# Attention denominators: weighted sums on ScalarE and GpSimd ahead of two matmul rounds, with M and the reciprocal moved later

## The chip, the cores and the metric

The kernel runs on one core of a Trainium2 chip. The metric is the device time of one execution in microseconds (us). A profile of one execution belongs to each kernel; it gives the busy time of each engine, the chain of work that ended last, and each instruction's start and duration. In its lines PE is TensorE's matmuls, PEld its weight loads, DVE is VectorE, ACT is ScalarE, POOL is GpSimd, SP is SyncE, which issues most DMAs, and SPq its DMA queue. L256 is line 256 of the kernel.

## What is computed

The input is x, 2048 tokens of 640 numbers in bfloat16. Two blocks are mixed by a gate per token:

```python
g = _sigmoid((x * gate_w).sum(-1, keepdims=True))
return g * a + (1 - g) * b
```

Block a is linear attention with 32 heads of 20 numbers. The change is in its denominators `den`:

```python
phi = lambda t: jnp.where(t > 0, t + 1, jnp.exp(t)) + 1e-6
pq, pk = phi(q), phi(k)
kv = jnp.einsum("bhsd,bhse->bhde", pk, v)
z = jnp.einsum("bhsd->bhd", pk)
num = jnp.einsum("bhqd,bhde->bhqe", pq, kv)
den = jnp.einsum("bhqd,bhd->bhq", pq, z)[..., None] + 1e-6
o = num / den
```

For every token and head, den is the sum over the head's 20 numbers of pq times z, where z is the sum of pk over all tokens. Block b is a mixer and an MLP: x1 = x + shift(gelu(layernorm(x) @ w1)) @ w2, then x1 + gelu(layernorm(x1) @ w3) @ w4. The shift moves the four quarters of the features by 1, -1, 2 and -2 tokens.

## The kernel before, in words

Nothing is reordered by a scheduler: each engine works its instructions in the order in which the program issues them, and waits by semaphores for what they need. So an instruction that waits holds up all that stand behind it on its engine. All matmul results go to PSUM through `pair()` (L71), a pool of four pairs of banks: a fifth matmul group waits until an earlier pair has been read out. The tokens are taken in 16 chunks of 128 or in four tiles of 512 (`NT`, `TS`). In order:

1. Keys (L206 to L234): k for each chunk, then phi into `pk`. Queries (`q_unit`, L237): q transposed, in five chunks j of 128 features, then phi into `pqT[:, j, :]`. Chunk j holds every fifth feature, so that a head's 20 numbers lie on four partitions of each of the five chunks.
2. `g_unit(j)` (L313), five units: 32 matmuls of `pk` with x give the product from which kv is made; the last column of the second half, `pt[:, 1, HD:HD + 1]`, is z for the 128 features of chunk j. ScalarE copies the product to `gs`; VectorE multiplies the mask `hmask` (which partition belongs to which head) with z into `zbd[:, j, :]`; SP transposes `gs` into `gT`. Between the units VectorE works out layernorm statistics (`ln1_stat`), GpSimd 1/sqrt of the variance (`ln1_rstd`, two instructions, L288 and L289), VectorE applies it (`ln1_apply`, L308), and SP transposes the result into `lnxT`, which W1 reads.
3. Two small memsets on GpSimd (L400, L401) write the first and last columns of `hsT`, then `w1_unit(0, ...)` (L347): three units, each of one or two chunks of W1 for tile 0, with a gelu on ScalarE (L356, L359) into `hsT`. The last unit's result is spread by four VectorE copies (L362).
4. `kv_unit` (L366) makes kv from `gT`, masked on VectorE into `kvT`. Then the first unit of W1 for tile 1, and the denominators: `den_mm` (L252) has 20 matmuls, five chunks by four tiles, with `zbd[:, j, :]` as 32-column weights; the four tiles go to four groups of 32 partitions. `den_evac` (L260) adds 1e-6 on VectorE, `den_recip` (L265) takes the reciprocal there.
5. `m_unit(g)` (L382), six units, M = kv times wo, copied out by ScalarE into `mst`, two of W1's units between them; `m_store` (L389) writes M to DRAM, and `m_load` reads it back in another arrangement into `m_sb`.
6. `w2_unit(0, cc)` (L428) for the four chunks of tile 0: ten matmuls, then VectorE adds x and takes statistics; `ln2_rstd` on GpSimd, `ln2_apply` (L448) on VectorE and a transpose on SP.
7. W1 for tile 2; after its first unit `r_spread` (L269): four VectorE copies and four DMAs that spread the reciprocals to all partitions (`rb`). Then `m_load`, the load of `w4_sb`, `scale_t(0)` (L275, VectorE multiplies pq of tile 0 by `rb`), W1 for tile 3, and the long rest: W3, W2, attention output (`att_unit`, L461) and W4 for tile after tile.

`xT` (x transposed) is read last by the queries. The pool that holds it, `st1`, is closed at L406, and the space is used again for `w4_sb` and others.

Of the kernel before, what the change touches and what calls it, by code (L numbers as in the profile page):

```python
# [7 lines left out]
ACT = mybir.ActivationFunctionType  # L8
# [8 lines left out]
def kernel(  # L17
# [14 lines left out]
    P = 128  # L32
# [57 lines left out]
    g5z = const.tile([P, P], BF16)  # L90
    mhalf = const.tile([P, CPT], F32)
    hmask = const.tile([P, H], F32)
    zbd = const.tile([P, DC, H], BF16)
    bmask = const.tile([P, GH * 4], F32)
    bmask5 = const.tile([P, 8], F32)
    ylog = const.tile([P, NCH], F32)
# [58 lines left out]
    for c in range(0, NCH, CPT):  # L155
# [3 lines left out]
                            base=0, pattern=[[-4, H]], channel_multiplier=1)  # L159
    nc.gpsimd.affine_select(out=hmask[:], in_=hmask[:], compare_op=ALU.is_ge, fill=0.0,  # L160
                            base=3, pattern=[[4, H]], channel_multiplier=-1)
    for m, n, off in ((bmask, GH, 0), (bmask5, 2, 88)):
        nc.gpsimd.memset(m[:], 1.0)
        nc.gpsimd.affine_select(out=m[:], in_=m[:], compare_op=ALU.is_ge, fill=0.0,
                                base=-off, pattern=[[-Dh, n], [0, 4]], channel_multiplier=1)
        nc.gpsimd.affine_select(out=m[:], in_=m[:], compare_op=ALU.is_ge, fill=0.0,
                                base=off + Dh - 1, pattern=[[Dh, n], [0, 4]], channel_multiplier=-1)
# [77 lines left out]
    def gate_ops():  # L245
# [3 lines left out]
        nc.vector.reciprocal(omg[:], omg[:])  # L249
        nc.vector.tensor_tensor(gate[:], gate[:], omg[:], op=ALU.mult)  # L250

    def den_mm():  # L252
        pt = pair()
        for j in range(DC):
            for t in range(NT):
                nc.tensor.matmul(pt[32 * t:32 * (t + 1), 0, :], lhsT=zbd[:, j, :], rhs=pqT[:, j, t * TS:(t + 1) * TS],  # L256
                                 start=(j == 0), stop=(j == DC - 1))
        return pt

    def den_evac(pt):  # L260
        d = x1p.tile([P, D], F32, name="x1")[:, 0:TS]
        nc.vector.tensor_scalar_add(d, pt[:, 0, :], 1e-6)
        return d

    def den_recip(d):  # L265
        with nc.allow_low_precision(reason="rounded after a float32 division, as a copy would"):
            nc.vector.reciprocal(r_bf[:], d)
# [28 lines left out]
    def ln1_stat(c):  # L296
        ln_stats(mv1[:, c, :], x_sb[:, c, 0:D], st1s[:, c])

    def ln1_rstd(t):
        tt = slice(t * CPT, (t + 1) * CPT)  # L300
        rsqrt(rstd1[:, tt], mv1[:, tt, 1])

    def ln1_apply(c):
        t, cc = divmod(c, CPT)
        if cc == 0:
            lnxT[t] = lnx_p.tile([P, DC, TS], BF16, name="lnxT")
        lnx = work.tile([P, D], BF16, name="ln")
        nc.vector.tensor_scalar(lnx[:], x_sb[:, c, 0:D], mv1[:, c, 0:1], rstd1[:, c:c + 1],  # L308
                                op0=ALU.subtract, op1=ALU.mult)
        nc.sync.dma_start_transpose(lnxT[t][:, :, cc * P:(cc + 1) * P], lnx[:])  # L310


    def g_unit(j):  # L313
        pt = pair()
        for c in range(NCH):
            w = pk[:, c, :].rearrange("p (m j) -> p j m", j=DC)[:, j]
            for hf in range(2):
                nc.tensor.matmul(pt[:, hf, 0:HD + hf], lhsT=w, rhs=x_sb[:, c, hf * HD:(hf + 1) * HD + hf],  # L318
                                 start=(c == 0), stop=(c == NCH - 1))
        nc.scalar.copy(gs[:, j % 2, :].rearrange("p (h e) -> p h e", h=2), pt[:, :, 0:HD])  # L320
        nc.vector.tensor_scalar_mul(zbd[:, j, :], hmask[:], pt[:, 1, HD:HD + 1])
        nc.sync.dma_start_transpose(gT[:, :, j * P:(j + 1) * P], gs[:, j % 2, :])

    for c in range(CPT):
        ln1_stat(c)
    ln1_rstd(0)
    g_unit(0)
    for cc in range(CPT):
        ln1_stat(CPT + cc)
        ln1_apply(cc)  # L330
    ln1_rstd(1)
    g_unit(1)
    for cc in range(CPT):
        ln1_stat(2 * CPT + cc)
        ln1_apply(CPT + cc)
    ln1_rstd(2)
    g_unit(2)
    for cc in range(CPT):
        ln1_stat(3 * CPT + cc)
    ln1_rstd(3)  # L340
    g_unit(3)
    g_unit(4)
    for cc in range(CPT):
        ln1_apply(2 * CPT + cc)

# [1 line left out]
    def w1_unit(t, fcs):  # L347
        pt = pair()
        for i, fc in enumerate(fcs):
            for dc in range(DC):  # L350
                w = w1_sb[:, dc, CG * fc:CG * fc + P] if fc < 4 else w1x[:, dc, :]
                nc.tensor.matmul(pt[:, i, :], lhsT=w, rhs=lnxT[t][:, dc, :], start=(dc == 0), stop=(dc == DC - 1))  # L352
        for i, fc in enumerate(fcs):
            if fc < 4:
                o = 2 + shifts[fc] + t * TS
                nc.scalar.activation(hsT[:, fc, o:o + TS], pt[:, i, :], ACT.Gelu_apprx_tanh)  # L356
            else:
                hx = hx_p.tile([P, TS], BF16, name="hx")
                nc.scalar.activation(hx[:], pt[:, i, :], ACT.Gelu_apprx_tanh)  # L359
                for g in range(4):  # L360
                    o = 2 + shifts[g] + t * TS
                    nc.vector.tensor_copy(hsT[32 * g:32 * (g + 1), 4, o:o + TS], hx[32 * g:32 * (g + 1), :])  # L362
# [3 lines left out]
    def kv_unit():  # L366
        pt = pair()
        for g in range(NG):
            n = heads[g] * Dh
            for fc in range(DC):  # L370
                nc.tensor.matmul(pt[:, g // 3, (g % 3) * GW:(g % 3) * GW + n], lhsT=wv_sb[:, fc, row0[g]:row0[g] + P],  # L371
                                 rhs=gT[:, fc, 0:D].rearrange("p (j h i) -> p j h i", j=DC, h=H)
                                 [:, :, head0[g]:head0[g] + heads[g], :], start=(fc == 0), stop=(fc == DC - 1))
        for bank, g0, g1 in ((0, 0, 3), (1, 3, 5), (1, 5, 6)):
            m, w = (bmask5, 8) if g0 == 5 else (bmask, 4 * GH)
            base, n = (g0 % 3) * GW, sum(heads[g0:g1]) * Dh
            nc.vector.tensor_tensor(
                kvT[:, g0 * GW:g0 * GW + n].rearrange("p (b a) -> p b a", a=w),
                pt[:, bank, base:base + n].rearrange("p (b a) -> p b a", a=w),
                m[:, 0:w].unsqueeze(1).broadcast_to([P, n // w, w]), op=ALU.mult)  # L380

    def m_unit(g):  # L382
        pt = pair()
        for hf in range(2):
            nc.tensor.matmul(pt[:, hf, 0:HD], lhsT=kvT[:, row0[g]:row0[g] + P],  # L385
                             rhs=wo_sb[:, g, hf * HD:(hf + 1) * HD], start=True, stop=True)
        nc.scalar.copy(mst[g // 2][:, g % 2, :].rearrange("p (h e) -> p h e", h=2), pt[:, :, 0:HD])

    def m_store():  # L389
        for i in range(NG // 2):  # L390
            nc.sync.dma_start(m_dram[2 * i:2 * i + 2].rearrange("g p e -> p g e"), mst[i])
# [9 lines left out]
    nc.gpsimd.memset(hsT[:, :, S:S + 4], 0.0)  # L401
    for fcs in w1_split:
        w1_unit(0, fcs)
    kv_unit()
    w1_unit(1, w1_split[0])
    s1.close()  # L406
    w4p = ctx.enter_context(tc.tile_pool(name="w4p", bufs=1))
    w4_sb = w4p.tile([P, FF + 1, D], BF16)
    h2x_p = ctx.enter_context(tc.tile_pool(name="h2x_p", bufs=2))
    h2p = ctx.enter_context(tc.tile_pool(name="h2p", bufs=1))  # L410
    x1p = ctx.enter_context(tc.tile_pool(name="x1p", bufs=11))
    den = den_evac(den_mm())
    mst = [x1p.tile([P, D], F32, name="x1")[:].bitcast(BF16).rearrange("p (g e) -> p g e", g=2) for _ in range(NG // 2)]
    for cc in range(CPT):
        ln1_apply(3 * CPT + cc)
    den_recip(den)
    for g in range(3):
        m_unit(g)
    w1_unit(1, w1_split[1])
    for g in range(3, 5):  # L420
        m_unit(g)
    w1_unit(1, w1_split[2])
    m_unit(5)
    m_store()
    st = {}


    def w2_unit(t, cc):  # L428
        c = t * CPT + cc
        if cc == 0:  # L430
            st[t] = dict(x1=[], mv=small.tile([P, CPT, 2], F32, name="mv2"))
        pt = pair()
        for hf in range(2):
            for fc in range(DC):
                nc.tensor.matmul(pt[:, hf, 0:HD], lhsT=hsT[:, fc, 2 + c * P:2 + (c + 1) * P],  # L435
                                 rhs=w2_sb[:, fc, hf * HD:(hf + 1) * HD], start=(fc == 0), stop=(fc == DC - 1))
        x1 = x1p.tile([P, D], F32, name="x1")
        nc.vector.tensor_tensor(x1[:].rearrange("p (h e) -> p h e", h=2), pt[:, :, 0:HD],  # L438
                                x_sb[:, c, 0:D].rearrange("p (h e) -> p h e", h=2), op=ALU.add)
        ln_stats(st[t]["mv"][:, cc, :], x1[:], small.tile([P, 2, 6], F32, name="bnst")[:])  # L440
        st[t]["x1"].append(x1)
# [146 lines left out]
            w4_store(t, cc, ocs[cc], *pts[cc, hf][1:])  # L588

    for cc in range(CPT):  # L590
        w2_unit(0, cc)
        ln2_rstd(0, cc, cc + 1)
        if cc >= 1:
            ln2_apply(0, cc - 1)
    for fcs in w1_split:
        w1_unit(2, fcs)
        if fcs[0] == 0:
            ln2_apply(0, CPT - 1)
            r_spread()
    m_load()  # L600
    nc.sync.dma_start(w4_sb[:, 0:FF, :], B_w4[0:FF * P, :].rearrange("(c p) f -> p c f", p=P))
    nc.sync.dma_start(w4_sb[0:FR, FF, :], B_w4[FF * P:F, :])
# [58 lines left out]
```

## Time and profile before

| | us |
|---|---|
| median of 3 runs | 263.09 |
| lowest, highest | 262.74, 263.66 |
| the profiled execution | 262.68 |
| its span, first to last instruction | 261.0 |
| TensorE busy in the span | 256.0 |
| VectorE busy | 141.4 |
| ScalarE busy | 93.5 |
| GpSimd busy | 27.9 |

The profiled execution has its own time beside its span, since some 1.7 us lie around the span. The groups of instructions have a mean duration each; those that the change touches or leans on:

| group | count | us each |
|---|---|---|
| L256 denominators' matmuls, 128x512, 32 weight columns | 20 | 1.19 in all |
| L320 ScalarE copy of g, 128x640 | 5 | 0.69 |
| L321 VectorE product with z, 128x32 | 5 | 0.24 |
| L308 VectorE layernorm apply, 128x640 bf16 | 16 | 0.42 |
| L289 GpSimd power, 128x4 | 4 | 1.05 |
| L170 GpSimd copies, 128x32 | 20 | 3.46 in all |
| L267 VectorE reciprocal, 128x512 | 1 | 3.35 |
| L385 matmuls of M, 128x320 | 12 | 1.73 in all |

Read the chain of work first: it says which engine's work, one piece after another, makes up the time. Then the timeline of an engine says when each instruction started, and in brackets how long the engine had been idle before it and what released it.

### The profile page before, as it was taken

Reading aid. Unit: us, or ns where it says so; the run is one execution under the profiler, and the core shown is the slowest. Engines: PE = TensorE matmul, PEld = TensorE weight load, DVE = VectorE, ACT = ScalarE, POOL = GpSimd, SP = SyncE. Lnnn points to the kernel's source line nnn. Section 1 sums busy time; section 2 is a strip of 40 time slices with the busy share of each in tenths; the row PEclk is TensorE's granted clock in tenths of the full one; section 3 lists DMA queues with packets and bytes.
Section 4 is the critical chain, followed back from the end, with each engine's and each line's share of the span. In section 5 each row is a group of like instructions: output and inputs, shape, how many; then the busy total and the mean of one; then the engine's idle time right before and its main releaser. Section 6 shows DMA issues by size and latency. Waiting matters only on the chain.

```text
span 261.0 us, 4113 instructions
## 1 busy us (share of the span) xinstructions
PE 256.0 (98%) x1601; PEld 151.5 (58%) x1625; DVE 141.4 (54%) x276; ACT 93.5 (36%) x144; POOL 27.9 (11%) x82
## 2 busy tenths in 40 slices
PE   8999999999999999999999999999999999999995
PEld 4677555688854644566464566455565546465543
DVE  2688778799947894876300398600287610125132
ACT  1655454321165446532343322342322344342100
POOL 3000050012220140131000131000023000000000
PEclk9999999999999999999999999999999999999999
DMA  7999996016684836994032123312123402211011
GB/s 206 204 147 378 365 338 242 0 28 121 122 107 82 216 65 133 186 311 88 14 43 40 20 52 90 81 23 57 23 50 73 102 20 43 43 44 54 24 50 53
DMA packets 57558, 28.28 MB, mean 108 GB/s; under 512 B 45506, under 2 KB 56770, under 8 KB 57538
## 3 DMA queue, kind: packets, MB, share of 16 engines
q1 hardware_dynamic: 57096, 27.52, 44.1%
q10 hardware_dynamic: 442, 0.49, 0.5%
q8 instruction: 13, 0.21, 0.4%
q14 instruction: 7, 0.06, 0.1%
HBM read 13.03 MB, written 3.60 MB: 64 GB/s over the span
## 4 chain that ended last, share of the span: by engine, by line
PE 98%; issue 1%; DVE 0%
PE pp L485 21%; PE pp L524 16%; PE pp L186 9%; PE pp L318 8%; PE pp L435 8%; PE pp L466 8%; PE pp L241 8%; PE pp L352 8%; PE pp L560 5%; PE pp L199 1%; PE pp L495 1%; PE pp L516 1%; PE pp L385 1%; PE pp L371 1%; PE pp L256 0%
## 5 line engine op out<-in xcount | busy, mean ns | idle before, releaser
L485 PE MATMUL pp<-lnxT,w_sb 128*128 128x512 bf16 x249 | 59.8, 379 | 0.6
L487 ACT ACTIVATE h<-pp 128x1024 bf16<-128x1024 f32 (+1 forms) x28 | 26.9, 962 | 56.0 <-PE pp L485 56.0
L524 PE MATMUL pp<-h,w_sb 128*128 128x512 bf16 (+1 forms) x228 | 42.4, 343 | 0.3
L485 PEld LDWEIGHTS <-w_sb 128*128 128x128 bf16 x260 | 25.2, 98 | 26.9
L438 DVE TENSOR_TENSOR x<-pp,x_sb 128x640 f32<-128x640 f32 x16 | 13.1, 817 | 42.7 <-PE pp L435 42.7
L524 PEld LDWEIGHTS <-w_sb 128*128 128x128 bf16 x234 | 22.7, 98 | 19.5 <-issue 1.0
L178 ACT ACTIVATE e<-pp 128x640 bf16<-128x640 f32 (+1 forms) x26 | 21.5, 827 | 9.5 <-PE pp L241 9.5
L466 PE MATMUL pp<-m_sb,pqT 128*128 128x320 bf16 x160 | 24.3, 299 | 0.0
L472 DVE SCALAR_TENSOR_TENSOR x<-pp,gate,x 128x640 f32<-128x640 f32 x16 | 14.1, 883 | 18.3 <-PE pp L466 12.6
L435 PE MATMUL pp<-w_sb,hsT 128*128 128x320 bf16 x160 | 23.9, 299 | 0.0
L186 PE MATMUL pp<-wk_sb,xT 128*128 128x320 bf16 (+1 forms) x160 | 23.0, 303 | 0.1
L288 POOL TENSOR_SCALAR rstd<-mv 128x1 f32<-128x1 f32 (+1 forms) x20 | 7.7, 385 | 142.1 <-DVE mv L294 142.1
L318 PE MATMUL pp<-x_sb,pk 128*128 128x320 bf16 (+1 forms) x160 | 22.0, 300 | 0.0
L241 PE MATMUL pp<-xT,hsT 128*128 128x512 bf16 x98 | 21.6, 379 | 0.1
L318 PEld LDWEIGHTS <-pk 128*128 128x128 bf16 x160 | 18.8, 117 | 3.2
L435 PEld LDWEIGHTS <-hsT 128*128 128x128 bf16 x160 | 15.6, 98 | 8.0
L466 PEld LDWEIGHTS <-pqT 128*128 128x128 bf16 x160 | 15.7, 98 | 7.7
L537 DVE SCALAR_TENSOR_TENSOR oc<-pqT,omg,x 128x640 bf16<-128x640 bf16 x12 | 10.5, 877 | 16.8 <-DMA pqT<-hx 16.8
L186 PEld LDWEIGHTS <-xT 128*128 128x128 bf16 x160 | 15.6, 99 | 6.9 <-DVE xT L215 0.9
L352 PE MATMUL pp<-lnxT,w_sb 128*128 128x512 bf16 x77 | 17.9, 379 | 0.2
L241 PEld LDWEIGHTS <-hsT 128*128 128x128 bf16 x100 | 11.8, 118 | 9.7
L528 ACT CAST hx<-pp 128x512 bf16<-128x512 f32 x12 | 7.0, 586 | 22.5 <-PE pp L524 14.9
(80 smaller groups left out, 236.6 us busy)
## 6 DMA issues: line engine op xcount, KB each, us to landing
x_sb<-in_A_x_dram SPq DMA_DIRECT2D x1, 2240.0 KB
out_dram<-oc SPq DMA_DIRECT2D x14, 160.0 KB, 1.9
w_sb<-in_B_w_dram SPq DMA_DIRECT2D x1, 2160.0 KB, 11.0
w_sb<-in_B_w_dram SPq DMA_DIRECT2D x1, 2080.0 KB
wo_sb<-in_A_wo_dram SPq DMA_DIRECT2D x6, 160.0 KB, 7.9
m_dram<-x SPq DMA_DIRECT2D x3, 320.0 KB, 5.0
hsT<-in_A_wqkv_dram SPq DMA_DIRECT2D x1, 800.0 KB
m_sb<-in_A_wqkv_dram SPq DMA_DIRECT2D x1, 800.0 KB
```

Source lines behind the costliest of these rows:

```text
L178: nc.scalar.activation(ev, src, ACT.Exp)
L186: nc.tensor.matmul(pt[:, hf, 0:n], lhsT=xT[:, dc, c * P:(c + 1) * P], rhs=wk_sb[:, dc, hf * HD:hf * HD + n], start=(dc == first), stop=(dc ...
L241: nc.tensor.matmul(pt[:, t % 2, :], lhsT=wq_sb[:, dc, :].rearrange("p (m j) -> p j m", j=DC)[:, j], rhs=xT[:, dc, t * TS:(t + 1) * TS], st ...
L318: nc.tensor.matmul(pt[:, hf, 0:HD + hf], lhsT=w, rhs=x_sb[:, c, hf * HD:(hf + 1) * HD + hf], start=(c == 0), stop=(c == NCH - 1))
L352: nc.tensor.matmul(pt[:, i, :], lhsT=w, rhs=lnxT[t][:, dc, :], start=(dc == 0), stop=(dc == DC - 1))
L435: nc.tensor.matmul(pt[:, hf, 0:HD], lhsT=hsT[:, fc, 2 + c * P:2 + (c + 1) * P], rhs=w2_sb[:, fc, hf * HD:(hf + 1) * HD], start=(fc == 0), ...
L438: nc.vector.tensor_tensor(x1[:].rearrange("p (h e) -> p h e", h=2), pt[:, :, 0:HD], x_sb[:, c, 0:D].rearrange("p (h e) -> p h e", h=2), op ...
L466: nc.tensor.matmul(pt[:, hf, 0:HD], lhsT=pqT[:, j, c * P:(c + 1) * P], rhs=m_sb[:, j, hf * HD:(hf + 1) * HD], start=(j == 0), stop=(j == D ...
L472: nc.vector.scalar_tensor_tensor(x1, pt[:, :, 0:HD], gate[:, c:c + 1], x1, op0=ALU.mult, op1=ALU.add)
L485: nc.tensor.matmul(pt[:, k, :], lhsT=w3_sb[:, dc, fc * P:(fc + 1) * P], rhs=lnT[:, dc, :], start=(dc == 0), stop=(dc == DC - 1))
L487: nc.scalar.activation(h2[:, 2 * i * TS:(2 * i + n) * TS], pt[:].rearrange("p h e -> p (h e)")[:, 0:n * TS], ACT.Gelu_apprx_tanh)
L524: nc.tensor.matmul(dst, lhsT=w4_sb[:, fc, d * P:(d + 1) * P], rhs=st[t]["h2"][:, fc * TS + a:fc * TS + b], start=False, stop=(fc == FF - 1))
```

## The change

The sum over the five chunks is taken off TensorE. For each chunk j, ScalarE multiplies pq's chunk by z, a number per partition, in two halves of 1024 tokens (`den_add`). The first goes into `u`, the others into `uz`, both float32 and laid over `xT`, and GpSimd adds `uz` to `u`. So `u` holds, on four partitions for each head, the sum over j. To feed it to TensorE in bfloat16 with little loss it is split: `den_hi` rounds `u` on ScalarE, `den_lo` takes the rest on VectorE. `den_mm` then sums over a head's partitions with the head mask in bfloat16, `hm_bf`, as weights: two parts by four tiles, eight matmuls.

`zbd` and its five products are gone; z is copied by ScalarE, ahead of the copy to `gs`. The first two adds follow unit 1 of g. The applies of layernorm for chunks 4 to 7 and the statistics of 8 to 15 are moved among the g units, so that SP's transposes of units 3 and 4 stand behind those of chunks 4 to 7. All W1 units of tile 1 now come before `den_mm`, `den_mm` before the pool is closed. Each of `m_unit(0..3)` stands ahead of a `w2_unit`, `m_unit(4)` and `m_unit(5)` around the first W1 unit of tile 2, and after them `m_store`, the last `ln2_apply` of tile 0, the reciprocal and `r_spread`. The two memsets of `hsT` stay where they were in the text, which is now behind the adds in GpSimd's queue.

```diff
+    halves = (slice(0, S // 2), slice(S // 2, S))
+    u = xT[:, 0:2, :].bitcast(F32).rearrange("p a s -> p (a s)")
+    uz = xT[:, 2:4, :].bitcast(F32).rearrange("p a s -> p (a s)")
+
+    def den_add(j):
+        for sl in halves:
+            nc.scalar.activation((uz if j else u)[:, sl], pqT[:, j, sl], ACT.Copy, scale=z[:, j:j + 1])
+            if j:
+                nc.gpsimd.tensor_tensor(u[:, sl], u[:, sl], uz[:, sl], op=ALU.add)
+
+    def den_hi(sl):
+        nc.scalar.copy(xT[:, 4, sl], u[:, sl])
+
+    def den_lo(sl):
+        nc.vector.tensor_tensor(xT[:, 3, sl], u[:, sl], xT[:, 4, sl], op=ALU.subtract)
+
     def den_mm():
         pt = pair()
-        for j in range(DC):
+        for n in range(2):
             for t in range(NT):
-                nc.tensor.matmul(pt[32 * t:32 * (t + 1), 0, :], lhsT=zbd[:, j, :], rhs=pqT[:, j, t * TS:(t + 1) * TS],
-                                 start=(j == 0), stop=(j == DC - 1))
+                nc.tensor.matmul(pt[32 * t:32 * (t + 1), 0, :], lhsT=hm_bf[:], rhs=xT[:, 4 - n, t * TS:(t + 1) * TS],
+                                 start=(n == 0), stop=(n == 1))
         return pt
...
+        nc.scalar.copy(z[:, j:j + 1], pt[:, 1, HD:HD + 1])
         nc.scalar.copy(gs[:, j % 2, :].rearrange("p (h e) -> p h e", h=2), pt[:, :, 0:HD])
-        nc.vector.tensor_scalar_mul(zbd[:, j, :], hmask[:], pt[:, 1, HD:HD + 1])
...
     g_unit(0)
+    den_add(0)
     for cc in range(CPT):
         ln1_stat(CPT + cc)
         ln1_apply(cc)
+    g_unit(1)
+    den_add(1)
     ln1_rstd(1)
-    g_unit(1)
     for cc in range(CPT):
         ln1_stat(2 * CPT + cc)
-        ln1_apply(CPT + cc)
+    g_unit(2)
+    den_add(2)
     ln1_rstd(2)
-    g_unit(2)
     for cc in range(CPT):
         ln1_stat(3 * CPT + cc)
+        ln1_apply(CPT + cc)
+    g_unit(3)
+    den_add(3)
+    g_unit(4)
+    den_add(4)
     ln1_rstd(3)
-    g_unit(3)
-    g_unit(4)
...
     nc.gpsimd.memset(hsT[:, :, S:S + 4], 0.0)
     for fcs in w1_split:
         w1_unit(0, fcs)
+    den_hi(halves[0])
     kv_unit()
+    den_lo(halves[0])
     w1_unit(1, w1_split[0])
+    den_hi(halves[1])
+    den_lo(halves[1])
+    w1_unit(1, w1_split[1])
+    w1_unit(1, w1_split[2])
+    den_ps = den_mm()
     s1.close()
...
-    den = den_evac(den_mm())
+    den = den_evac(den_ps)
...
-    den_recip(den)
-    for g in range(3):
-        m_unit(g)
-    w1_unit(1, w1_split[1])
-    for g in range(3, 5):
-        m_unit(g)
-    w1_unit(1, w1_split[2])
-    m_unit(5)
-    m_store()
...
     for cc in range(CPT):
+        m_unit(cc)
         w2_unit(0, cc)
         ln2_rstd(0, cc, cc + 1)
         if cc >= 1:
             ln2_apply(0, cc - 1)
-    for fcs in w1_split:
+    m_unit(4)
+    w1_unit(2, w1_split[0])
+    m_unit(5)
+    m_store()
+    ln2_apply(0, CPT - 1)
+    den_recip(den)
+    r_spread()
+    for fcs in w1_split[1:]:
         w1_unit(2, fcs)
-        if fcs[0] == 0:
-            ln2_apply(0, CPT - 1)
-            r_spread()
```

## The prediction

> **What bounds the kernel now.** I read the page's first and fourth parts, then the chain in order of time, then the timelines of ScalarE, GpSimd and VectorE around the change.
>
> ```profile
> span 261.0 us, 4113 instructions
> PE 256.0 (98%) x1601; PEld 151.5 (58%) x1625; DVE 141.4 (54%) x276; ACT 93.5 (36%) x144; POOL 27.9 (11%) x82
> PE 98%; issue 1%; DVE 0%
> ```
>
> TensorE bounds it: 98% of the chain is matmuls. A matmul removed is time gained, and any wait that TensorE gets is time lost; there is almost none to hide it in. The chain around the change:
>
> ```profile
> 71.27 5.13 PE pp L352 x23
> 76.40 1.44 PE pp L371 x30
> 77.84 0.22 PE pp L352
> ...
> 80.00 1.19 PE pp L256 x20
> 81.20 0.92 PE pp L385 x6
> ```
>
> The reader is to see the order first W1 tile (71.0), kv (76.40), second W1 tile (77.84), denominators (80.00), M (81.20), with no gap between them. What lets TensorE run on at 77.84 is on two other engines:
>
> ```profile
> 62.22 1.05 POOL L289 TENSOR_TENSOR rstd<-rstd,mhalf 128x4 f32<-128x4 f32 x1
> ...
> 73.36 0.12 POOL L400 MEMSET hsT<- 128x20 bf16 x1
> 73.39 1.28 ACT L356 ACT_TABLE_LOAD   x1
> ...
> 74.69 2.06 ACT L356 ACTIVATE hsT<-pp 128x512 bf16<-128x512 f32 x4
> ```
>
> The first gelus of W1 (74.69) write columns of hsT that the two memsets (73.36) also write, so they wait for the memsets. GpSimd works its queue in order: whatever is put ahead of the memsets delays the gelus. The gelus empty the PSUM pair that the second W1 tile needs at 77.84 (four pairs: first W1 tile takes three, kv the fourth). So the memsets have a slack of about 77.84 - 1.09 (two gelus) - 73.5 = 3.2 us.
>
> **The change, part by part.**
>
> *TensorE.* 20 matmuls at L256 took 1.19 us (four column groups side by side, so five rounds); eight remain, two rounds: 1.19 x 2/5 = 0.48, a gain of 0.7. M's twelve matmuls are moved, not changed.
>
> *ScalarE.* Ten weighted copies of 128x1024. Nearest rows: four 128x640 copies with a scale took 2.97 us (L459, 0.74 each), and L487 takes 1.02 at 1024 columns against 0.60 at 512, 0.82 ns a column; so 0.74 + 384 x 0.82 ns = 1.05 us each. ScalarE has 3.8 us of work between 49.2 and 71.0, so 2.1 per unit of 4.36 fits. hi adds two such copies.
>
> *GpSimd.* Eight adds of 128x1024 f32, which no row shows. The rows that vary in width:
>
> ```profile
> 1.10 0.29 POOL L153 TENSOR_SCALAR_AFFINE_SELECT ident<-ident 128x128 bf16<-128x128 bf16 x1
> ...
> 1.68 0.21 POOL L158 TENSOR_SCALAR_AFFINE_SELECT hmask<-hmask 128x32 f32<-128x32 f32 x1
> ```
>
> (0.29 - 0.21)/96 = 0.83 ns a column for one input. Lower bound: one input's price, 0.19 + 1024 x 0.83 ns = 1.04 us. Upper bound: the w1x copies, 3.46 us for 20 of 32 columns, 5.4 ns a column if all of it grew with width: 5.5 us. I take two inputs at the select's price, 1.70, plus the fixed part of GpSimd's two-input instruction (L289: 0.58 at one column, 1.05 at four, so 0.42): **2.1 us**, near the selects because only they show a slope over enough columns.
> The Trainium skill, GPSIMD Engine Reference, section 3.1, speaks against this edit: it gives 4497 ns for an f32 add of 2048 columns and says to leave elementwise work to VectorE. Half of that is 2.25 us, by which the sum below would be 1.2 us higher; no run here shows it yet.
>
> *The queue on GpSimd.* The first add needs unit 1 of g: its matmuls end at 57.9, then z (0.2), gs (0.69) and a weighted half (1.05): 59.9. From there GpSimd is never idle, since the halves come every 4.36 us and two adds with an rstd take 5.6. In order: eight adds 16.8; three rstd pairs (61.83 to 63.27 = 1.44 each) 4.3; the memsets 0.2. A further term is VectorE:
>
> ```profile
> 92.13 0.58 DVE L452 TENSOR_SCALAR ln<-x,mv,rstd 128x640 bf16<-128x640 f32 x1
> 92.30 0.49 POOL L288 TENSOR_SCALAR rstd<-mv 128x1 f32<-128x1 f32 x1 [0.96 <-DVE mv L294]
> ```
>
> At 90.45 the same L288 took 0.23; here it ends at 92.79, just after VectorE's L452 (92.71), and so at 94.69 and 97.08 too. An apply on VectorE holds GpSimd up. Eight applies (0.39 to 0.45 each) fall among the adds: 0 to 3.5 us, I take 2.5.
> The Trainium skill, SBUF — State Buffer, "Who interferes with whom", has it in both directions: the second to start waits for the whole of the first. The trace agrees for GpSimd waiting; that VectorE would wait 2 us for an add no row here shows.
> If VectorE does wait, the applies of chunks 4 to 7 end late (71 becomes about 77); SP transposes gT(3) and gT(4) behind them (1.25 each), and kv, which needs both, starts near 83 instead of 76.4. That lies inside the wait below: the memsets come later still.
>
> *The sum.* 59.9 + 16.8 + 4.3 + 2.5 + 0.3 = 83.8 for the memsets' end; two gelus 1.09: 84.9 where TensorE wanted 77.84: **+7.1**. Behind the gelus on ScalarE stand hi, and behind hi the gelus of the second tile. After 84.9: three gelus 1.6, hi 1.05, two gelus 1.09, hi 1.05 make 89.7, and lo on VectorE (128x1024, two inputs; L180 takes 1.23 at that size) 91.0. TensorE is at the second half of the denominators at 84.9 + 5.4 + 0.2 = 90.5: **+0.5**. TensorE **-0.7**. Clock: in the first 5 us of the kernel a 512-column matmul took 0.43 us (six in 2.61) against 0.216 later, and full rate came about 5 us after the first. If a long wait brings that back, up to 2.5 us more, of which 1 lies beside the wait for the gelus: 0 to 1.5, I take **+0.7**. The last transpose before W3 now sits behind the M stores on SP and the late applies: **+0.1**. Together +7.7.
>
> *Edits at nothing, and their cover.* The five zbd products (0.24 each) leave VectorE, which was busy 20.4 of 21.8 us there; hm_bf's copy falls into 29 us of idle GpSimd. The reciprocal (3.35 on VectorE) leaves 83.28 and now stands before r_spread: the row of r's copies (98.77, 3.7 before W3's first matmul) comes about 2.5 us later against TensorE. Cover: scale_t ended at 106.8, the first att_unit ran at 113.0, 6.2 us; the W4 load is issued at 105.39, takes 11 to 12, and is needed at 127.9, 10 us. Beyond that each us costs a us. M between the w2 units takes PSUM pairs, but as built the pairs that M takes are those that w2 has freed two units earlier; VectorE needs 2.4 us per w2 unit, TensorE now 1.63, and four pairs last until W1's third tile as before (91.66). If M_3 had to wait for the first w2 sum, up to 1.5 us.
>
> **Rivals.**
> 1. *Adds at one input's price, 1.04 us.* GpSimd keeps up with the g units; the last add waits for unit 4 (71.0 + 1.9 = 73.0), then two adds and an rstd: memsets at 76.6, gelus out at 77.8. No wait at 77.84. What stays is kv waiting 0.3 for gT(4), lo 0.3, W3 0.2, less 0.7: **262.8**; if VectorE is held up by adds, kv is 2 us late: 264.4. For it: selects of 8 to 32 columns all take about 0.2, so fixed cost dominates and I may overrate the second input. Against: two 4-byte inputs.
> 2. *The other side: faster.* As rival 1, but all three small waits hidden: TensorE's 0.7 is all that counts, **262.0**. It decides only from adds of at most 1.1 us that do not hold VectorE up. For it: the chain is all TensorE. Against: the slack at kv is already about 0.3 (its weight load idles 0.31) and SP now puts four transposes ahead of gT(3).
> 3. *Adds without VectorE's exclusion* (that term 0, idle 4.6 us at the second W1 tile): 82.4 instead of 84.9, the clock's term up to 1.4: 262.7 + 4.6 + 0.5 - 0.7 + 1.0 = **268.1**.
> 4. *Adds of 3.4 us or more* (four times the bytes per column of the select): each 0.1 us more is 0.8 in all: 262.7 + 7.7 + 8 x 1.3 = **281**.
>
> **How the numbers follow.** The profiled execution took 262.68 us (span 261.0), the median of three is 263.09, and the sum is made on 262.68: 262.68 + 7.7 = **270.4**. Chances: forecast (268.5 to 274) 0.52, rival 3 0.18, rival 1 0.14, rival 4 0.11, rival 2 0.05. The range reaches from rival 1's upper case to adds of 2.6 us (11.5 more): **263.5 to 275.0**, which leaves out rival 2, half of rival 1 and rival 4, some 0.22. Faster by over 0.3% (0.8 us, about what a measurement of this kernel can tell from no change) is part of rival 2, 0.04; within 0.3% the rest of it and half of rival 1, 0.09; slower 0.87.
>
> **What would show it.** Right: the adds at about 2.1 us back to back from 60 on; the memsets at 80 to 85; the first gelu right behind them and the table load long done; a gap of 5 to 8 us on TensorE ahead of kv or the second W1 tile; applies that end with an add. Wrong: adds near 1 us, memsets before 77, or a first gelu ahead of the memsets, which would take the forecast's main term away; a wait of TensorE later, at w2 or att, would be a term that I set at nothing.

## The result, and the profile after

The changed kernel took 273.25 us (median of 4 runs, 272.81 to 273.48) against 262.91 for the kernel before in the same comparison (4 runs, 262.68 to 263.66): a ratio of 1.0386, with a 95% interval of 1.0361 to 1.0411. The profiled execution took 273.17 us, with a span of 271.5. The page of the kernel after, its span, its busy times, its chain by engine and its row of granted clock:

```profile
span 271.5 us, 4144 instructions
PE 259.6 (96%) x1613; PEld 152.9 (56%) x1613; DVE 152.4 (56%) x273; ACT 107.1 (39%) x161; POOL 47.0 (17%) x91
...
PEclk9999999999995999999999999999999999999999
...
PE 78%; DVE 15%; DMA 2%; issue 1%; ACT 1%; POOL 1%; SPq 0%; DVEq 0%; POOLq 0%
```

The chain was 98% matmuls and is now 78%, with 15% on VectorE. TensorE is busy for 3.6 us more although the denominators have twelve matmuls less (the trace of before lacks some matmul records, so that 3.6 is rather too much), and the row of granted clock has a 5 in its thirteenth slice, where it was 9 all along. So there are two things to look for: waits of TensorE, and matmuls that run at half rate. TensorE's timeline after, where the bracket is the idle time before a group:

```profile
75.28 1.24 PE L375 MATMUL pp<-lnxT,w1x 128*128 128x512 bf16 x5
82.61 2.82 PE L394 MATMUL pp<-wk_sb,m_sb 128*128 128x120 bf16 x30 [6.08 <-issue]
85.26 5.79 PE L375 MATMUL pp<-lnxT,w_sb 128*128 128x512 bf16 x20
...
92.06 0.61 PE L274 MATMUL pp<-xT,hm_bf 128*32 128x512 bf16 x8
...
112.76 2.33 PE L506 MATMUL pp<-lnxT,w_sb 128*128 128x512 bf16 x10 [2.12 <-DMA lnxT<-ln]
```

Two waits are all there is: 6.08 ahead of kv, and 2.12 ahead of W3. kv's thirty matmuls took 1.59 in before's timeline and take 2.82, at half rate or near it; the next twenty, which in the full-rate kernels below take 4.48, take 5.79. The denominators take 0.61 where before's timeline has 1.26.

These make the whole difference. kv starts 6.4 us later than before (82.61 against 76.25 in before's timeline); from its start to that of the second W1 tile it takes 1.2 more (2.65 against 1.44); these twenty matmuls 1.3 more; the denominators 0.65 less; W3 waits 2.1. That is 6.4 + 1.2 + 1.3 - 0.65 + 2.1 = 10.4; the profiled executions are 10.5 apart and the medians 10.3.

Why kv waits shows on other engines. VectorE's timeline after, its layernorm applies:

```profile
59.09 0.39 DVE L326 TENSOR_SCALAR ln<-x_sb,mv,rstd 128x640 bf16<-128x640 bf16 x1
...
60.44 2.07 DVE L326 TENSOR_SCALAR ln<-x_sb,mv,rstd 128x640 bf16<-128x640 bf16 x1
...
75.66 6.91 DVE L326 TENSOR_SCALAR ln<-x_sb,mv,rstd 128x640 bf16<-128x640 bf16 x5
```

GpSimd's timeline after, its first two adds, its last four, and the first memset:

```profile
59.97 4.77 POOL L262 TENSOR_TENSOR xT<-xT 128x1024 f32<-128x1024 f32 x2 [2.31 <-ACT xT L260]
...
72.15 9.53 POOL L262 TENSOR_TENSOR xT<-xT 128x1024 f32<-128x1024 f32 x4
...
83.07 0.11 POOL L423 MEMSET hsT<- 128x20 bf16 x1
```

The same apply takes 0.39 before the first add and 2.07 after it has begun; it ends at 62.51, and the first of the two adds, 4.77/2 = 2.39 long, at 62.36. A page counts such an instruction as busy: 16 applies have a mean of 1.02 now and 0.42 before, so that some 9 of VectorE's 11 us more are waiting, not work. The applies of chunks 4 to 7, the last of which is the first of the five at 75.66, hold up SP's queue. SyncE's DMA queue after:

```profile
71.00 7.33 SPq L328 DMA_TRANSPOSE lnxT<-ln  x4
78.42 2.55 SPq L340 DMA_TRANSPOSE wk_sb<-gs  x2
...
107.06 1.94 SPq L414 DMA_DIRECT2D m_dram<-x  x3
109.09 1.37 SPq L475 DMA_TRANSPOSE lnxT<-ln  x1
```

The transposes of chunks 4 to 7 are spread over 7.33 us, since each waits for its apply; behind them stand gT(3) and gT(4), issued from 78.42 to 80.97, and kv needs both: it starts at 82.61, 1.64 after the last of them was issued. The second wait has the same form: M's three stores stand on SP ahead of the last transpose that W3 reads. That transpose is issued at 109.09, though its apply had ended at 106.65.

### The profile page after: what moved, and what is told of

Its sections match the earlier page's. It is cut to its first block, busy times and chain, and to the rows that moved or that the text cites. A ratio compares the mean times of both kernels' runs of the same rounds, so it can differ in the third digit from the quotient of the medians.

```text
span 271.5 us, 4144 instructions
## 1 busy us (share of the span) xinstructions
PE 259.6 (96%) x1613; PEld 152.9 (56%) x1613; DVE 152.4 (56%) x273; ACT 107.1 (39%) x161; POOL 47.0 (17%) x91
## 4 chain that ended last, share of the span: by engine, by line
PE 78%; DVE 15%; DMA 2%; issue 1%; ACT 1%; POOL 1%; SPq 0%; DVEq 0%; POOLq 0%
PE pp L506 21%; PE pp L545 16%; PE pp L188 8%; PE pp L487 8%; PE pp L243 8%; PE pp L456 6%; PE pp L581 5%; DVE ln L326 4%; DVE st1s L311 2%; DVE st1s L310 2%; PE pp L375 2%; DMA lnxT<-ln 1%; DVE mv L312 1%; DVE x L459 1%; PE pp L394 1%
## 5 line engine op out<-in xcount | busy, mean ns | idle before, releaser
L506 PE MATMUL pp<-lnxT,w_sb 128*128 128x512 bf16 x260 | 60.4, 379 | 2.1 <-DMA lnxT<-ln 2.1
L558 DVE SCALAR_TENSOR_TENSOR oc<-pqT,omg,x 128x640 bf16<-128x640 bf16 x12 | 10.5, 877 | 16.8 <-DMA pqT<-hx 16.8
L375 PE MATMUL pp<-lnxT,w_sb 128*128 128x512 bf16 x80 | 19.4, 398 | 0.0
L262 POOL TENSOR_TENSOR xT<-xT 128x1024 f32<-128x1024 f32 x8 | 19.0, 2397 | 2.3 <-ACT xT L260 2.3
```

Source lines behind the costliest of these rows:

```text
L262: nc.gpsimd.tensor_tensor(u[:, sl], u[:, sl], uz[:, sl], op=ALU.add)
L506: nc.tensor.matmul(pt[:, k, :], lhsT=w3_sb[:, dc, fc * P:(fc + 1) * P], rhs=lnT[:, dc, :], start=(dc == 0), stop=(dc == DC - 1))
```

## The experiments

In the first batch (x1 to x4) the kernel before took 262.91, in the second (x5 to x8) 262.81, in the third (x9 to x11) 262.68, in the last 262.74; each ratio is to that of its batch, with its 95% interval.

**x1: the memsets ahead of the adds.** The forecast had TensorE wait for gelus behind the memsets. Here they leave that place:

```diff
+    nc.gpsimd.memset(hsT[:, :, 0:4], 0.0)
+    nc.gpsimd.memset(hsT[:, :, S:S + 4], 0.0)
     (after ln1_rstd(0); removed ahead of w1_unit(0, ...))
```

> The changed kernel with the two memsets of hsT issued ahead of the adds on GpSimd. Theory 1 (transposes): TensorE restarts when gT(3) and gT(4) land, and they stand on SP behind the transposes of chunks 4 to 7, whose applies on VectorE the adds hold up. Then kv still starts near 82.6 and the second W1 tile near 85.2, and the time stays at 272.8 to 273.4, though the first gelu comes about 4 us earlier (79.4). Theory 2 (memsets, the main term of the prediction's sum): the gelus behind the memsets set the restart, and with them gone from the end of the queue most of 7 us goes: 266 to 269.

Measured: 273.67, ratio 1.0419 [1.0376, 1.0463]: no gain. The gelus ran at 79.55 instead of 83.22, and TensorE's timeline has the wait where it was:

```profile
82.75 2.83 PE L396 MATMUL pp<-wk_sb,m_sb 128*128 128x120 bf16 x30 [6.09 <-ACT hx L384]
```

The bracket names ScalarE's last gelu, but that had ended at 82.10. SyncE's queue shows what came last:

```profile
78.56 2.55 SPq L340 DMA_TRANSPOSE wk_sb<-gs  x2
```

The last transpose is issued at 81.11, and kv starts 1.64 later, as in the changed kernel. So the wait in front was not that for the memsets. It was kv's wait for the transposes. Below, a gate is what TensorE has to wait for at one place: kv's gate is the transposes, and that of the second W1 tile is the gelus behind the memsets.

**x2: without the adds.** The eight GpSimd adds are left out, all else stays:

```diff
-            if j:
-                nc.gpsimd.tensor_tensor(u[:, sl], u[:, sl], uz[:, sl], op=ALU.add)
```

> The changed kernel without GpSimd's eight adds (u holds chunk 0 only, so the denominators lack four fifths of their sum). Theories 1 and 2 both have the adds at the root: the applies take 0.4 us again, gT(4) lands about 1 us after kv could start, memsets near 73, no drop of the clock; only the wait before W3 (2.1) stays: 263.0 to 265.5. Theory 3 (the moved steps on SP, VectorE and ScalarE cost this by themselves): 268 or more.

Measured: 266.38 (264.77 to 267.46), ratio 1.0115 [1.0072, 1.0157], more than expected. All applies were back at 0.39 to 0.45, and kv waited 0.55:

```profile
76.96 1.59 PE L392 MATMUL pp<-wk_sb,m_sb 128*128 128x120 bf16 x30 [0.55 <-PE pp L373]
```

So the adds account for about 6.9 of the 10.3 us, and 3.5 stay without them. In the profiled execution W3 waited 2.64 and then ran its first ten matmuls in 3.22 instead of 2.33. Executions with a mean granted clock of 0.994 took 267.0 to 267.5, those at 1.0 took 264.8 to 265.7.

**x3: M stored behind the last ln2 apply.**

```diff
-    m_store()
     ln2_apply(0, CPT - 1)
+    m_store()
```

> The changed kernel with the M stores behind the last apply of tile 0 on SP, not ahead of its transpose. If the stores on SP hold the last transpose (its apply ended at 106.65, it was issued at 109.09), the wait of 2.1 us before W3 goes whole: 271.0 to 271.5. If VectorE's chain of sums and applies decides, 0.5 us or less goes: 272.7 to 273.2.

Measured: 271.74, ratio 1.0342 [1.0317, 1.0366]: 1.5 less than the changed kernel. W3's wait is gone, so SP's queue made it; but it did not give back all of 2.1, because the next wait came up. TensorE's timeline:

```profile
121.52 1.52 PE L487 MATMUL pp<-m_sb,pqT 128*128 128x320 bf16 x10 [1.23 <-DVE bnst L311]
```

The first attention unit, which waited for nothing in the changed kernel, now waits 1.23. So the waits together give 2.12 - 1.23 = 0.9. Of the 1.8 between the two profiled executions another 0.8 lies ahead of the edit and has nothing to do with it: the twenty matmuls of the second W1 tile took 4.95 here and 5.79 there, so the half rate ended sooner in this execution.

**x4: TensorE kept busy while kv waits.** 28 matmuls of 512 columns go into kv's PSUM pair ahead of kv, which overwrites them.

```diff
     pt = pair()
+    warmup(28, TS, pt)
```

> The changed kernel with 28 matmuls of ones (128x512, about 6.05 us) on TensorE between the first W1 tile and kv, where it waits, into kv's own PSUM pair ahead of its start. If the half rate after the wait comes from TensorE's idleness, kv takes 1.44 in place of 2.82 us and the first two units of W1's second tile 4.32 in place of 5.64; the gelus' gate at 84.3 takes 0.4 of that back: 270.6 to 271.2. If the rate has another cause, the time stays at 273.0 to 273.5.

Measured: 270.85, ratio 1.0306 [1.0289, 1.0324], 2.4 less with more matmuls, and a mean granted clock of 1.0. TensorE's timeline:

```profile
82.08 1.60 PE L395 MATMUL pp<-wk_sb,m_sb 128*128 128x120 bf16 x30
83.96 4.48 PE L375 MATMUL pp<-lnxT,w_sb 128*128 128x512 bf16 x20 [0.28 <-ACT hsT L379]
```

Both groups are back at before's durations, and the second W1 tile at once waits 0.28 for gelus: at full rate the gate of the memsets is only a quarter of a microsecond behind that of the transposes.

**x5: without the adds, and M stored late (x2 and x3 together).**

> The changed kernel without GpSimd's eight adds (denominators lack four fifths of their sum) and with the M stores behind the last apply of tile 0. If adds and stores are the two causes, what is left is kv's wait of 0.5, less 0.7 for the denominators' matmuls: 262.5 to 263.5, no different from before. If the moved reciprocal, M or W2 order cost more, 264.5 or more.

Measured: 264.41 (9 runs), ratio 1.0065 [1.0047, 1.0083], more than expected though the adds are left out and W3 does not wait. What stays of the waits is kv's 0.55 and the first attention unit's 0.88; less 0.65 for the denominators that makes 0.8, and the profiled execution (263.70) is 0.9 above before. The median is another 0.7 higher, which this profile doesn't explain. So the change without its adds and without its store on SP would still not be faster than before.

**x6: the moves alone.** The kernel before, with its own 20 denominator matmuls and products with z; only W1's units of tile 1, M, the store, the reciprocal and its spread stand in the changed order. The edit, shortened:

```diff
+        m_unit(cc)                      (ahead of each w2_unit(0, cc))
+    m_unit(4); w1_unit(2, w1_split[0]); m_unit(5)
+    m_store()
+    ln2_apply(0, CPT - 1)
+    den_recip(den); r_spread()
```

> The kernel before, denominators by the old 20 matmuls, with only M, the stores, the reciprocal and the spread moved as in the changed kernel. If the order on SP (stores ahead of the last transpose) costs the wait before W3 by itself: 1.5 to 3 us and a half rate after it in some executions, 264.5 to 267. If that wait needs the late start that the adds bring, it stays at 262.7 to 263.3.

Measured: 264.9, ratio 1.007 [1.0046, 1.0095]. TensorE's timeline has the wait of the changed kernel to the hundredth, without any of the new denominators:

```profile
104.38 2.33 PE L479 MATMUL pp<-lnxT,w_sb 128*128 128x512 bf16 x10 [2.12 <-DMA lnxT<-ln]
```

**x7: adds of 512 columns.** Twice as many adds of half the width, so that VectorE, if it waits for the add that runs, waits for a shorter one.

```diff
-                nc.gpsimd.tensor_tensor(u[:, sl], u[:, sl], uz[:, sl], op=ALU.add)
+                for a in range(sl.start, sl.stop, S // 4):
+                    nc.gpsimd.tensor_tensor(u[:, a:a + S // 4], u[:, a:a + S // 4], uz[:, a:a + S // 4], op=ALU.add)
```

> The changed kernel with each GpSimd add split in two of 512 columns. If VectorE's apply waits for the whole GpSimd instruction that is running, its longest duration falls from 2.46 to about 1.3 us. If it waits for GpSimd's queue or for data, it stays above 2. Sixteen adds of 1.25 us keep GpSimd about 1 us longer: 272.5 to 274.5 in time under both.

Measured in a single execution: 274.17, as both theories had it. The longest single apply fell from 2.46 to 1.42, so VectorE does wait for the running add and no longer:

```profile
67.89 1.42 DVE L327 TENSOR_SCALAR ln<-x_sb,mv,rstd 128x640 bf16<-128x640 bf16 x1
```

TensorE's timeline:

```profile
78.87 1.59 PE L395 MATMUL pp<-wk_sb,m_sb 128*128 128x120 bf16 x30 [2.15 <-issue]
85.93 0.58 PE L376 MATMUL pp<-lnxT,w_sb 128*128 128x512 bf16 x1 [5.47 <-ACT hsT L380]
```

kv waited 2.15 instead of 6.08. But the second W1 tile then waited 5.47 for its gelus: the adds now took 1.28 each, 20.5 in all instead of 19.0, and the memset came at 84.64. The time went from one gate to the other.

**x8: the applies of chunks 4 to 7 on ScalarE.** They no longer meet the adds on VectorE; GpSimd makes minus mean times rstd for them. The main line of the edit:

```diff
+            nc.scalar.activation(lnx[:], x_sb[:, c, 0:D], ACT.Identity, bias=nmr[:, cc:cc + 1], scale=rstd1[:, c:c + 1])
```

> The changed kernel with the applies of chunks 4 to 7 on ScalarE, so that GpSimd's adds can't hold them up and gT(3), gT(4) are transposed in time. If two gates stand side by side, kv starts near 77 but the second W1 tile still waits for the gelus behind the memsets (84.3): 271.5 to 273.5. If the transposes were the only gate: 266 to 268.

Measured: 274.01, ratio 1.0441 [1.0379, 1.0504]. TensorE's timeline shows the same exchange:

```profile
79.39 1.59 PE L401 MATMUL pp<-wk_sb,m_sb 128*128 128x120 bf16 x30 [1.64 <-issue]
86.15 0.59 PE L382 MATMUL pp<-lnxT,w_sb 128*128 128x512 bf16 x1 [5.18 <-ACT hsT L386]
```

kv waits 1.64, and the memsets, at 84.87 here, make the rest. (The profiled execution took 276.91, the slowest of four: its first W1 tile started 1.2 later than in the changed kernel, and half rate after both long waits cost some 4.) The 1.64 seem to come from chunks 0 to 3: two of their applies still waited for the first adds (2.07 and 1.45), their transposes took SP 7.98 instead of the 5.25 of x2, and from there on SP's queue has no gap up to the last transpose that kv needs.

**x9: x8 and x1 together.** Either alone had changed nothing.

> The changed kernel with both gates opened: ScalarE makes the applies of chunks 4 to 7, so that SP's transposes are not late, and the two memsets stand ahead of the adds on GpSimd. Either one alone left the time at 273.7 and 274.0. Two-gate theory: kv starts near 79.4 as with the applies on ScalarE (a wait of 1.6 instead of 6.1), and the second W1 tile then waits only for two gelus that stand on ScalarE behind the last weighted half (79.94), the table load (1.28) and themselves (1.1), so 82.4 against 81.0, a wait of 1.4. With W3's wait of 2.1 and TensorE's 0.7 less that makes 1.6 + 1.4 + 2.1 - 0.7 = 4.4 over the kernel before: 267.3, up to 268.7 if the clock halves after W3's wait. Rival, that one of the two gates is the only cause and the other edit is idle: 273 to 274 as before.

Measured: 268.75, ratio 1.0235 [1.0203, 1.0266], about 5 less than either. TensorE's timeline:

```profile
78.14 1.59 PE L403 MATMUL pp<-wk_sb,m_sb 128*128 128x120 bf16 x30 [1.63 <-issue]
81.15 4.48 PE L384 MATMUL pp<-lnxT,w_sb 128*128 128x512 bf16 x20 [1.41 <-ACT hsT L388]
...
107.75 3.85 PE L513 MATMUL pp<-lnxT,w_sb 128*128 128x512 bf16 x10 [2.32 <-DMA lnxT<-ln]
```

The waits of 1.6 and 1.4 are those worked out in advance. Both gates were there, one behind the other; the third wait, at W3, is as before and brought half rate in this execution (3.85 instead of 2.33).

**x10: all gates opened.** x9, with M stored behind the last apply, the rstd of chunks 12 to 15 ahead of the last adds, and the last weighted halves behind the first W1 unit's gelus. Part of the edit:

```diff
+    ln1_rstd(3)
     g_unit(4)
...
     w1_unit(0, w1_split[0])
+    den_add(4)
```

> As the kernel with both gates opened, and besides: the rstd of chunks 12 to 15 goes ahead of the last adds, the last weighted halves stand behind the first W1 unit's gelus on ScalarE, and M is stored behind the last ln2 apply. My theory: kv waits 1.6, the second W1 tile nothing, the denominators 0.4 to 0.8 for the low part, W3 nothing, the first attention unit about 1 for M read back later, and TensorE saves 0.7: 262.8 + 2.4 = 265.2, between 264.4 and 266. Rival, that the change's whole price is the two gates and W3: what is left is kv's 1.6 less 0.7, 263.8 or less. If it is under 262.5, the change gains once its waits are gone.

Measured: 266.77, ratio 1.0152 [1.013, 1.0173]: the best form of the change with all its work in it, 6.5 less than the change as made, and 1.6 above what I expected. kv's wait (1.63) and the attention unit's (1.09) are as expected; the miss is at the denominators. TensorE's timeline:

```profile
85.18 0.40 PE L275 MATMUL pp<-xT,hm_bf 128*32 128x512 bf16 x4 [0.38 <-DVE kvT L408]
86.22 0.39 PE L275 MATMUL pp<-xT,hm_bf 128*32 128x512 bf16 x2 [0.64 <-DVE xT L269]
87.35 0.39 PE L275 MATMUL pp<-xT,hm_bf 128*32 128x512 bf16 x2 [0.74 <-DVE xT L269]
```

VectorE's timeline, ahead of the low parts at 84.95:

```profile
79.85 4.21 DVE L393 COPY hsT<-hx 32x512 bf16<-32x512 bf16 x4 [1.77 <-ACT hx L390]
```

Four copies that otherwise take 1.19 take 4.21 beside the last adds, which end at 83.31; kv's masking and then the low parts stand behind them. With every gate open, the adds still make the denominators late, here through VectorE's copies.

**x11: the moves alone, with M stored behind the last apply.** x6 with the swap of x3.

> The kernel before with only M, its store, the reciprocal and its spread moved as in the change, and M's store behind the last ln2 apply; the denominators are made as before. The moves with the store first took 264.9, with a wait of 2.12 at W3. If SP's queue is all that these moves cost, 262.8. If the later M costs at the first attention unit, as it did without the adds (0.88), 263.7.

Measured: 264.1, ratio 1.0057 [1.0039, 1.0076]. W3 waits no more. VectorE's timeline and TensorE's:

```profile
107.96 1.49 DVE L277 TENSOR_TENSOR pqT<-pqT,rb 128x2560 bf16<-128x2560 bf16 x1 [3.88 <-DMA m_sb<-m_dram]
```

```profile
114.28 1.52 PE L460 MATMUL pp<-m_sb,pqT 128*128 128x320 bf16 x10 [1.06 <-DVE bnst L293]
```

The scaling of pq stood at 105.30 in the kernel before. It is 2.66 later, and VectorE then works without a gap (copies, sums of W2, statistics) until 114.2, where the first attention unit starts. The releaser in the bracket of the first line is the last that the trace saw; the chain of waits of this kernel goes through the reciprocal, the copies and the DMAs of r.

**x12: the same without the reciprocal**, to tell whether it or the late M is what attention waits for.

```diff
-            nc.vector.reciprocal(r_bf[:], d)
+            nc.vector.tensor_copy(r_bf[:], d)
```

> The kernel before with M, its store behind the last ln2 apply, the reciprocal and its spread moved as in the change, but with the reciprocal left out: a plain copy (some 0.4 us instead of 3.35 on VectorE) stands in its place, so that attention is multiplied by the denominators instead of divided by them. With the reciprocal this kernel took 264.1, and its first attention unit waited 1.06. My theory is that the reciprocal, on VectorE right ahead of the spread of r, makes the first scaling of pq 2.7 later, and with it all that stands behind it on VectorE: then r is spread 2.9 earlier, the wait is gone, and the time is 262.7 to 263.2. Rival, that the late M (stored and read back later) is what the attention unit waits for: the wait stays at 0.8 to 1.1, and the time at 263.8 to 264.2.

Measured: 263.4 (12 runs), ratio 1.0026 [1.0005, 1.0046], between what the two theories gave. SyncE's queue and TensorE's timeline:

```profile
99.73 1.45 SPq L391 DMA_DIRECT2D m_dram<-x  x3
101.28 3.15 SPq L273 DMA_DIRECT2D rb<-r  x4
104.52 2.81 SPq L397 DMA_DIRECT2D m_sb<-m_dram  x6
```

```profile
113.28 1.52 PE L460 MATMUL pp<-m_sb,pqT 128*128 128x320 bf16 x10 [0.44 <-DMA m_sb<-m_dram]
```

r was copied by 99.54, 3.3 earlier than in x11, but its DMAs then stood on SP behind M's store, and went out only 1.6 earlier. So the reciprocal makes about 0.6 of the 1.06, and M's late place on SP the 0.44 that stay. Whether those 0.44 end with r or with M's read-back the trace doesn't separate.

No kernel of these is faster than the kernel before. Those with the whole change's work in them lie between 266.8 and 274.2.

## Why the prediction was right, and where it was not

The forecast was 270.4 in a range of 263.5 to 275.0, and slower; the time is 273.25. The cause, the adds on GpSimd with queues behind them, held: without them (x2) 6.9 of 10.3 us are gone. The signs set in advance came as well: the memsets at 83.07, a gap of 6.08 ahead of kv, applies that end with an add. But the number came as near as it did partly by luck, since errors of both signs cancelled. Step by step:

- **The adds.** 2.1 forecast from slopes of other instructions, 2.38 measured (19.0 for the eight, against 16.8). From x7, 1.28 at 512 columns: (2.38 - 1.28)/512 = 2.1 ns a column and 0.2 fixed, where I had 1.66 and 0.4. The Trainium skill, GPSIMD Engine Reference, section 3.1, was nearer, by an estimate: half of its 4497 ns for 2048 columns is 2.25.
- **VectorE's exclusion.** This failed as put: "An apply on VectorE holds GpSimd up", 2.5 us on GpSimd's chain. Among the adds it went the other way. Adds follow each other every 2.34 to 2.39 us, so GpSimd lost next to nothing, and applies of 0.39 took up to 2.46. The Trainium skill, SBUF — State Buffer, "Who interferes with whom", has the lock in both directions; the trace now agrees for VectorE too (2.07 against 0.39). The two errors on GpSimd's chain, 2.2 too little for the adds and 2.5 too much for the lock, cancelled by luck: the memsets' end at 83.8 forecast, 83.2 measured.
- **The main wait, +7.1.** The size held (6.4), the place did not. I had kv's start "near 83" (82.61 measured), and wrote of this wait for gT that it "lies inside the wait below". The gelus that wait for the memsets let the second W1 tile go at 83.22 + 1.09 = 84.31; kv, had it run at its old 1.44, would have let it go at 82.61 + 1.44 = 84.05. The two gates were 0.26 apart (x4: 0.28), so either alone left nothing to gain (x1, x8), and both together gave about 5 (x9). In the changed kernel it was kv's, since kv ran at half rate.
- **The clock, +0.7.** Mis-sized: 2.5 measured in the profiled execution (1.2 on kv, 1.3 on W1), 2.4 taken away by x4. It varies: the same wait cost W1 0.2 in x1's profile (4.64 for the twenty matmuls) and 0.5 in x3's (4.95), so 1.4 to 2.5 in all. I laid part of the slow time beside the wait for the gelus; but the long wait stood ahead of kv, so kv's own half rate came on the path too.
- **W3's transpose, +0.1.** The step that failed most: 2.12 measured. I named the place, M's stores ahead of it on SP, and priced it at almost nothing. M's three stores took 1.94 of the queue, right when the last apply was done. x6 shows the same 2.12 without any new denominators, x3 and x11 take it away.
- **The edits at nothing.** "6.2 us" of cover for the later reciprocal were counted from the scaling of pq to the first attention unit. Between the two, VectorE has four copies and sums of W2 to make, and 2.66 later became a wait of 1.06 (x11), so the true cover was 1.6 at most. In the changed kernel W3's wait hid it; in x3 and x10 it came out (1.23, 1.09).
- **lo, +0.5.** No wait in the changed kernel, since all of TensorE was later. In x10, where it was not, the low parts cost 1.4.
- **TensorE, -0.7.** Right: 1.26 became 0.61.
- **The rivals.** Rival 3 was right that no apply holds GpSimd's chain up, but with its adds at 2.1 it ended the gelus at 82.4, where 84.3 was measured, and it had nothing for W3. Rivals 1 and 2 needed adds of 1.1 us or less, rival 4 adds of 3.4 or more.

By the measured terms: 6.4 + 2.5 + 2.1 - 0.65 = 10.4 where I had 7.7. The main wait and lo came 1.2 under the forecast, the clock 1.8 and W3 2.0 over it.

## What to carry to other kernels

When an edit delays two chains that meet at one engine, work out the end of each: the later one sets the time, and mending one alone can show nothing (x1 and x8: no gain, x9: 5 us). Of an instruction moved on a DMA queue ask what stands behind it, and take its own length as the price if that is due at once: three stores of 1.9 us cost 2.1. Here a gain of 0.65 us on the bounding engine did not pay for 19 us of adds on another, whose result came too late even with every gate open (x10).

## What the runs showed of the hardware

- While a 128x1024 float32 add runs on GpSimd, a bfloat16 apply on VectorE waits for its end: 2.07 instead of 0.39, and up to 2.46; with adds of half the width, up to 1.42. The page counts this waiting as busy. Statistics on VectorE beside the adds kept their time (0.48 with or without an add), copies did not (four in 4.21 instead of 1.19).
- A wait of 6.1 us on TensorE was followed by half rate in each profile that has it without filler matmuls (kv 2.82 or 2.83 instead of 1.59), and so were the waits of 5.47 in x7 and 5.18 in x8 (the next eighteen matmuls of W1 in 4.99 and 6.11, where twenty take 4.48). Waits of 2.1 to 2.7 at W3 were followed by it in some profiles (x1 after 2.15, x2 after 2.64, x8 after 2.39, x9 after 2.32) and not in others (the changed kernel and x6 after 2.12, x7 after 2.66). The Trainium skill, TensorE: Matmul & The Clock Gate, Part 1, puts the drop to half rate after an idle window of about 3.4 us; here 2.15 was enough in one profile, and 2.66 was not in another.
